# The 64-row halves of a contraction ordered one by one, in an attention and gated-MLP block

## The chip, the cores and the metric

The kernel runs on one core of a Trainium2 chip. The metric is the device time of one execution in microseconds (us), and lower is better. Before the change three executions took 269.1, 269.65 and 269.99 us; the median is 269.65.

The engines have short names in the profile. PE is the matrix engine (PEld is its loading of weights), ACT does activations and copies, DVE and POOL do vector work, and SP issues most of the DMAs. An engine works through its own instructions in order and waits on semaphores for the others.

## The reference

The computation is one transformer block with 2048 positions (S) of width 448 (D): sliding-window attention with 16 heads of 28, and then a gated MLP whose gate mixes positions.

```python
mod = silu(c) @ w_mod                     # six vectors: sa, ca, ga, sb, cb, gb
h = layernorm(x) * (1 + ca) + sa
q, k, v = split(h @ wqkv)                 # 16 heads of 28
p = softmax(q @ k.T * 28 ** -0.5)         # window of 256, causal
x = x + ga * ((p @ v) @ wo)
h = layernorm(x) * (1 + cb) + sb
z = gelu(h @ w_in)                        # 1792 wide: z1 and z2, 896 each
g = w_sp @ layernorm(z2) + b_sp           # w_sp is 2048 x 2048
x = x + gb * ((z1 * g) @ w_out)
```

What matters here is that three products contract over D = 448: Q, K and V from `wqkv`, z1 and z2 from `w_in`. 448 is three times 128 and one half of it, 64.

## The kernel before

**How 448 rows lie in 128 partitions.** The transposed activations `hT` and the weights are kept in four chunks of 128 rows that start at rows 0, 128, 192 and 320 (`CH`). Chunks 1 and 2 overlap by 64 rows. A product over all 448 rows takes chunks 0 and 3 whole, and then either chunk 1 whole with the upper half of chunk 2 (rows 64 to 127), or chunk 2 whole with the lower half of chunk 1 (rows 0 to 63). So each contraction is three matmuls of 128 rows and one half of 64.

**Two ways to do the half.** For Q, K and V the function `project` (line 775) makes, with its inner `chain`, four matmuls of 128 rows each; the half's other 64 weight rows are set to zero (`z_v`, `z_wq`), so that the fourth matmul is a padded full one. For z1 and z2 the class `Pair` (line 734) takes two contractions together, one of either kind, does six full matmuls, and one operation `rest` that issues both halves one behind the other: one on rows 64 to 127 and one on rows 0 to 63 of the array (`tile_position` (64, 0) and (0, 0)). There are 30 such pairs: 16 for z2 (448 columns, one pair per tile of 128 positions) and 14 for z1 (512 columns).

**Tile sizes on PE.** A matmul uses the array as one 128x128 tile, as two of 64x128 (the halves), as four of 32x128 (the scores, of which each head contracts 28 rows) or as four of 128x32 (the product of probabilities and V, called PV). `Planner.column_tiles` (line 104) turns runs of full matmuls that stand next to 128x32 work into four 128x32 matmuls each: an operation of mode `FREE` can stand either way, a 64-row one can't and ends a run.

**The order.** The kernel describes its work as about 1,700 operations, each with the engines that may do it, what it depends on and the buffers it needs. `Planner.schedule` (line 81) doesn't decide anything when the kernel is built: it reads the order, the engine of each operation and its buffer from a stored string (`ORDER`, line 177). A token `135/2` is operation 135 with its second free buffer choice, `.1` behind a number takes the operation's second option. `emit` then makes one instruction stream and the semaphore waits for each engine.

**The stages.** (1) Loads, layer norm, the modulation vectors; x is normed, transposed and modulated into `hT` in six blocks of 1, 1, 2, 4, 4 and 4 tiles (`BLOCKS`); blocks 0 to 2 are transposed on PE, blocks 3 to 5 by DMA from SP's queue (`transp_dma`, line 705). (2) Attention over 16 query tiles. For each there are up to three groups of 16 score matmuls (S, line 457 through `mm`), each followed by two exponentials on ACT of about 1 us (line 908), a mask on POOL (line 914) for two of three groups, PV on PE, the normalisation, and the output product with `wo`. Q, K and V of the later blocks fill PE's time between score groups, and ACT and DVE share their copies out of PSUM (lines 806, 809, 818, 821). The first z2 tiles (`zraw`, tiles 0 to 4) are also computed in this stage and copied (lines 1008, 1011). (3) z1 and z2 with their gelus on ACT and the norm of z2 on DVE and POOL. (4) The product with `w_sp` (named G here; parts of four matmuls of 512 columns), whose transposes come by DMA through SP's queue, the gating on DVE, and the output product with `w_out`. The last operation is `fin` on DVE (line 1128) and the store.

Nearly all matmuls carry line 457, and those that were split into four carry line 454, because all go through the helper `mm`.

Of the kernel before, what the change touches and what calls it, by code (L numbers as in the profile page):

```python
# [11 lines left out]
FREE, COLS, WHOLE = 128, 33, 129  # L12
# [28 lines left out]
class Op:  # L41
    __slots__ = ("name", "prio", "opts", "deps", "order", "tens", "table", "dma", "seq", "mode", "port", "accs",
                 "hold", "pair", "scores", "eng", "fn", "start", "end", "avail", "token", "extra", "pending")
# [12 lines left out]
class Planner:  # L56
# [9 lines left out]
    def op(self, name, prio, opts, deps=(), tens=(), table=None, dma=None, order=(), mode=None, port=False, accs=(), hold=500, pair=None):  # L66
        o = Op()
        o.hold, o.pair, o.scores = hold, pair, 0
        o.name, o.prio, o.opts = name, prio, opts
        o.deps, o.order, o.tens = list(flat(deps)), list(flat(order)), list(flat(tens))  # L70
        o.table, o.dma, o.mode, o.port, o.accs = table, dma, mode, port, list(flat(accs))
        o.eng, o.token, o.extra = None, None, []
        o.seq = len(self.ops)
        self.ops.append(o)
        for t in o.tens:
            t.users.append(o)
        for a in o.accs:
            a.ops.append(o)
        return o

    def schedule(self):

        for tok in ORDER.split():
# [12 lines left out]
            o.eng, _, o.fn = o.opts[int(opt or 0)]  # L96
            for a in o.accs:
# [80 lines left out]
15 0 28 23 36 35 1 2 3 21 1684/0 24 22 33 34 37/6 38 4 8 67 68 27 32 1685 1686 25 1687 1688 1689 1690 39 1691 26 69 70 6 71/2 74/7 1692 31 40/6 41 42  # L178
43 44 45 63.2 1693 1694 1695 1696 1697 1698 46 47 48 62.2 58.1 49 50 65.1 51 52 53 11 54 125 60.1 55 56 78/2 79 1699 1700 75 1701 126 127 1702 7 61
76/1 5 72/6 73.1 1703 77 1704 1705 128 95/2 129 130.1/2 85/6 86 10 90/7 12 91 180 57.1 92 96 97 87 88 93 182 181 80/4 81 98 82 94 9 99 64.2 83 183  # L180
133/1 131/3 132.1 89 59.2 84 115/4 184 134 105/5 106 107 100/6 101 13 108 109 249 14 66.1 116 117 118 30.1 119 140/1 141 142 143 247 144 250 185 186
18 188.1/0 496/0,0 498/4 135/2 136 137 138 139.1 165/3 166 167 168 102 103 104 150/1 151 152 153 155/2 156 157 158 110/1 19 111 112 113 17 145/0 146
169 160/3 161 251 147 148 154 170/1 162 163 114 245 159 497/1,1 252 190/2 248 246 253 16 149 171 187.1/4 328 20 332 254 255 164 192/3 501/8 172 173
174 189 259/3 191.1 193 194 257.1/1 120/6 121 122 123 124 513/0,1 514/5 175/1 176 517/7 258.1/0 177 178 179.1 515 333 494/3 411 215/0 216 217 218 219
256.1/4 195/2 196 197 198 199 225/1 226 227 228 229 495 520/0,1 523/2 230/0 521/9 231 232 233 234.1 220/1 221 222 205/2 206 207 208 209.1 200/3 334
263 223 502 503/0 201 202 203 29 204 499 500 504/0 210/2 211 335 261 224 505 534/1,0 518 262 330 535/10 212 213 214.1 538/3 240/3 241 242 243 235/1
236 260 244.1 264 267 516/0 265 237 238 519 524 239 266 331 541/0,1 506.1/0 329 336 522 542/2 525/0 526 337 338 340.1/1 415 268/2 545/6 323/1 324 269
278/3 279 280 281 282 344 416 546 342.1/4 346 325 326 536 548/1,0 549/4 551/1 339.1/2 327.1 270 271 341.1/3 507/0 527.1/0 288/3 289 543 343 272.1 290
417 303/0 291 304 305 306 562/0,1 566/5 292.1 563/9 413 273/1 274 275 276 283/2 539 284 285 286 307.1 277 287.1 308/3 309 569/0,1 570/8 310 311 312.1
298/1 299 300 301 418 576/0,2 547/0 540 573/7 567 537 544 552 550 302.1 293/1 414 294 577/0 564 579/1 295 296 590/1,0 528/2 553/0 554 529/0 530 531  # L190
591/4 532 297.1 508/1 509 510 511 597/1,2 594/6 571 533 580/0 568 574 598/10 575 565 572 578 345 555.1/0 556/2 601/0 512 557/1 581/0 582 348.1 558 559
604/0,1 560 561 349.1 347.1 376/0 350.1 377 378 592 583.1/0 379 380.1 361/1 605/8 618/2,0 362 363 928 959 364 607/5 595 584/2 599 619/2 381/0 622/3
382 383 384 625/2,1 365.1 412 419 366/1 367 960 368 369 602 385.1 606/0 600 626/9 420 421 423.1/2 425.1/1 370.1 596 593 603 608 609/0 610 926 929
632/2,0 627 927 629/7 635/5 633/6 611.1/0 429 427 585/1 586 587 588 356/0 646/0,1 589 963 357 650/10 318/1 647/4 422.1/3 319 320 321 322.1 358 359
360.1 653/1,2 396/1 612/2 397 398 399 400.1 943/0 944 945 946 947 948 949 950 657/1 620 660/2,0 957 313/1 951 424.1/4 654/8 314 315 316 648 961 623
624/0 621 636 634 661/0 674/1,2 317.1 663/3 658 630 631 628 962 351/1 352 353 651 354 637/0 655 656/0 662 652 638 426 639.1/1 678/7 681/2,0 675/5 676
682/0 664 659 685/1 428 432.1 430.1 649 355.1 371/1 372 373 374 665/0 688/2,1 689/6 640/1 641/0 642 643 433.1 644 683 375.1 386/1 387 388 389 958
691/9 702/2,0 706/10 645 401/0 402 403 390.1 679 703/3 404 406/1 407 408 709/0,1 964 965 966 409 405.1 613/0 614 615 616 710/4 410.1 666 454/1 455
1419 716/0,2 431 456 457 686 931 967 713/2 974/1 617 680/0 687 980 692 719/8 677 684 936 690 975 717/9 458.1 730/1,2 667.1/0 693/0 707 694 391/1 392
932 393 394 933 395.1 970/2 449/0 450 451 668/1 938 452 453.1 731/7 737/1,0 732 464/1 981 465 466 467 468.1 968/0 734/6 735 669/0 670 671 672 741/1  # L200
744/0,2 969 695.1/1 704 444/1 673 445 446 733/0 738/0 747/5 745/7 447 448.1 736 748 758/2,1 696/0 742 743 434/1 982 762/6 739 935 1423 740 759/0 746
714 435 436 437 749/0 750 763 751.1/0 711 765/1,0 769/7 770 697/0 698 699 700 1421 438.1 937 766/1 459/1 460 461 701 986 972/1 772/0,2 773/5 705/0 720
718 708 715 712 767 775/9 462 987 786/0,1 721/0 439/0 440 441 442 971 790/4 463.1 479/1 480 481 793/2,1 722 723.1/1 443.1 771/0 768 482 774 764 760
791 724/2 984 761 776 787/10 794/3 800/2,0 797/8 803/7 483.1 484/1 985 485 486 939 487 788 983 988 989 777/0 778 488.1 469/0 470 471 472 814/1,0 752/0
753/1 473.1 941 801/1 754 755 756 818/5 821/0,2 795 779.1/1 973 815/0 979 976.1 725/0 726 727 728 825/9 757 798 780/1 781/1 990 782 783 784 819 822/6
1005 828/2,1 831/2 729 804/0 792 816 785 474/1 475 476 477 1003 1004 826 993/2 823 829/4 842/1,0 846/7 930 942 1007 478.1 934 940 789 843/10 977.1 799
802 796 805/0 952/1 849/0,2 850/1 1008 1420 832/0 820 830 853/4 806 807.1/1 953 827 817 824 833/0 856/0,1 978.1 851 1072/0 1074 1073 997/0 1056/2
857/2 995/1 847 854 994 808/1 809/3 810 811 812 1058 956 859/8 1057 991/2 870/1,0 871/5 1422 955 872 954 1076/1 1077 834 1075 813 1078 1062/3 874/0
# [989 lines left out]
```

## Time and profile before

| | |
|---|---|
| executions | 269.1, 269.65, 269.99 us |
| span of the profiled execution, first to last instruction | 267.2 us |
| median over that span (the profiled execution's time outside the span isn't shown separately) | 2.45 us |
| PE busy | 258.8 us (97%), 3059 matmuls |
| ACT, DVE, POOL busy | 133.2, 166.0, 103.8 us |
| granted PE clock | 1.0 of full speed throughout |
| DMA | 23.83 MB |

A busy time is a share of the whole span, an average over stages. The views that the prediction uses are: the busy times; the chain that ended last (followed back from the last instruction, with start and length of each piece); the busy times of each engine in stretches of the span; the timeline, which lists runs of equal instructions with their start; and the groups, with the number of instructions, their busy time and the mean of one. A matmul's listed duration contains its way through the array; the next one can start long before it ends, so what a matmul costs is read from the distance of starts.

### The profile page before, as it was taken

What the parts mean: (1) busy time and instruction counts of PE and PEld (TensorE: products, weight loads), DVE (VectorE), ACT (ScalarE), POOL (GpSimd) and SP (SyncE); (2) the same over time, 40 slices, a digit from 0 to 9 for tenths busy, and PEclk for the clock granted to TensorE, in tenths of its full rate; (3) what the DMA queues carried; (4) which work ended last, traced back from release to release, by engine and by line L of the source; (5) the groups of instructions that cost most, each with busy time, mean ns of one, the idle gap of its engine ahead of it and who ended that gap; (6) DMA issues with size and microseconds to landing.
All of it is one profiled execution on the core that took longest, in us unless ns stands there. A gap on an engine that the chain in (4) does not pass through costs nothing.

```text
span 267.2 us, 7093 instructions
## 1 busy us (share of the span) xinstructions
PE 258.8 (97%) x3059; PEld 127.8 (48%) x3059; DVE 166.0 (62%) x389; ACT 133.2 (50%) x182; POOL 103.8 (39%) x163
## 2 busy tenths in 40 slices
PE   6799999999999899999999999999999999999996
PEld 2676455554554444544444444444444444444553
DVE  4789987878789999488888730722033071327553
ACT  4899899999999999977687100000000000000100
POOL 3774799997989866436532300000000000000000
PEclk9999999999999999999999999999999999999999
DMA  6974260371998341789799950000000000000133
GB/s 225 352 194 56 42 178 5 71 122 23 172 212 195 65 100 39 124 118 164 157 191 215 165 97 0 2 0 0 0 0 2 0 0 0 2 0 17 52 101 108
DMA packets 61020, 23.83 MB, mean 89 GB/s; under 512 B 49854, under 2 KB 60861, under 8 KB 60989
## 3 DMA queue, kind: packets, MB, share of 16 engines
q1 hardware_dynamic: 60715, 22.92, 41.0%
q8 instruction: 24, 0.39, 0.7%
q10 hardware_dynamic: 274, 0.46, 0.5%
q14 instruction: 7, 0.06, 0.1%
HBM read 9.47 MB, written 1.84 MB: 42 GB/s over the span
## 4 chain that ended last, share of the span: by engine, by line
PE 76%; ACT 14%; DMA 3%; DVE 3%; SPq 1%; POOL 1%; issue 1%
PE ps L457 71%; ACT PT L908 12%; PE ps L454 5%; DMA wqk_raw<-in_A_wqkv_dram 2%; DMA hT<-xn 2%; ACT QKT L806 1%; DVE w_out_sb L964 1%; POOL PT L914 1%; ACT hT L683 1%; SPq L488 1%; DVE oq L940 1%; DVE oT L949 0%; PE ps L772 0%; POOL xn L620 0%; SPq L505 0%
## 5 line engine op out<-in xcount | busy, mean ns | idle before, releaser
L908 ACT ACTIVATE PT<-ps 128x1024 bf16<-128x1024 f32 x90 | 84.5, 1059 | 2.3 <-PE ps L457 1.7
L1037 ACT ACTIVATE z1T<-ps 128x512 bf16<-128x512 f32 x28 | 15.1, 599 | 100.9 <-PE ps L457 100.8
L1106 DVE TENSOR_TENSOR tmpg<-ps,bsp_bc 128x512 bf16<-128x512 f32 x28 | 18.8, 688 | 60.9 <-PE ps L457 60.6
L457 PE MATMUL ps<-QKT,z 128*128 128x512 bf16 x224 | 50.0, 379 | 0.0
L914 POOL TENSOR_SCALAR_AFFINE_SELECT PT<-PT 128x512 f32<-128x512 f32 x60 | 36.8, 635 | 5.1 <-ACT PT L908 5.1
L457 PEld LDWEIGHTS ps<-QKT,z 128*128 128x128 bf16 x224 | 21.9, 98 | 26.4 <-ACT z2raw L1018 0.2
L607 POOL TENSOR_TENSOR rs_all<-ve_all,neghalf 128x1 f32<-128x1 f32 (+2 forms) x27 | 18.6, 692 | 27.8 <-DVE ve_all L606 26.7
L457 PE MATMUL ps<-w_spC,z 128*128 128x512 bf16 x112 | 25.8, 379 | 0.0
L457 PE MATMUL ps<-w_spD,z 128*128 128x512 bf16 x112 | 25.8, 379 | 0.0
L457 PE MATMUL ps<-hT,w_in_sb 128*128 128x512 bf16 (+1 forms) x101 | 25.2, 380 | 0.0
L457 PE MATMUL ps<-w_in_sb,hT 128*128 128x448 bf16 (+1 forms) x110 | 24.4, 353 | 0.4 <-DVE oq L940 0.2
L620 POOL TENSOR_SCALAR xn<-x_sb,rs_all,nm_all 128x512 bf16<-128x512 bf16 x26 | 20.2, 782 | 4.7 <-DVE nm_all L611 3.0
L457 PE MATMUL ps<-w_out_sb,z1T 128*128 128x448 bf16 (+2 forms) x119 | 21.9, 341 | 0.0
L457 PE MATMUL ps<-hT,WQK 128*128 128x512 bf16 (+2 forms) x123 | 21.1, 307 | 0.7 <-ACT QKT L806 0.7
L599 DVE BATCH_NORM_STATS2 st_all<-x_sb 128x6 f32<-128x448 bf16 x32 | 19.3, 615 | 3.0 <-DMA x_sb<-in_A_x_dram 2.8
L599 DVE BATCH_NORM_STATS2 st_all<-z2raw 128x6 f32<-128x448 bf16 x32 | 19.3, 618 | 2.1 <-ACT z2raw L1018 1.8
L457 PE MATMUL ps<-QKT 28*128 28x128 bf16 x720 | 18.3, 217 | 1.5 <-ACT PT L908 1.4
L457 PEld LDWEIGHTS ps<-QKT 28*128 28x128 bf16 x720 | 10.4, 92 | 15.6 <-ACT PT L908 11.3
L809 DVE CAST QKT<-ps 128x512 bf16<-128x512 f32 (+2 forms) x26 | 16.1, 624 | 2.8 <-PE ps L457 1.8
L457 PEld LDWEIGHTS ps<-w_spC,z 128*128 128x128 bf16 x112 | 10.9, 98 | 13.4 <-DVE ve_all L606 0.4
L457 PEld LDWEIGHTS ps<-w_spD,z 128*128 128x128 bf16 x112 | 11.0, 98 | 13.2
L457 PEld LDWEIGHTS ps<-w_out_sb,z1T 128*128 128x128 bf16 x119 | 11.6, 98 | 9.9
(93 smaller groups left out, 319.3 us busy)
## 6 DMA issues: line engine op xcount, KB each, us to landing
wmod_sb<-in_w_mod_dram SPq DMA_DIRECT2D x8, 224.0 KB, 4.3
w_in_sb<-in_B_w_in_dram SPq DMA_DIRECT2D x8, 224.0 KB, 4.3
out_dram<-fin SPq DMA_DIRECT2D x16, 112.0 KB, 1.7
x_sb<-in_A_x_dram SPq DMA_DIRECT2D x3, 448.0 KB, 6.6
bsp_bc<-in_B_b_sp_dram SPq DMA_DIRECT2D x1, 512.0 KB, 4.7
wqk_raw<-in_A_wqkv_dram SPq DMA_DIRECT2D x1, 452.0 KB, 5.6
wmod_sb<-in_w_mod_dram SPq DMA_DIRECT2D x1, 448.0 KB, 4.5
wmod_sb<-in_w_mod_dram ACTq DMA_DIRECT2D x1, 448.0 KB, 4.8
```

The source lines that it names most:

```text
L454: last = e.matmul(out_[32 * j:32 * j + 32], lhsT=lhsT[:, 32 * j:32 * j + 32], rhs=rhs, start=st, stop=sp, tile_position=(0, 32 * j), **kw)
L457: return e.matmul(out_, lhsT=lhsT, rhs=rhs, start=st, stop=sp, **kw)
L488: return load(name, prio, lambda e: e.dma_start(x_sb[:, t0:t0 + n, :], x_d[:, t0:t0 + n, :]), n * 128 * D * 2, order=order)
L599: st = [dve("%sst%d" % (name, i), prio, dve_ns(D), lambda e, i=i, s_=s_: e.bn_stats(st_all[:, slot, t, i, :], s_()), deps, tens) for i, s_ ...
L607: r = pool(name + "rs", prio, 420 + 148 * n, lambda e: e.tensor_tensor(rs_all[:, slot, t0:t1], ve_all[:, slot, t0:t1], neghalf[:, t0:t1], ...
L620: return e.tensor_scalar(dst, src, rs_all[:, slot, t:t + 1], nm_all[:, slot, t:t + 1], ALU.mult, ALU.add)
L683: last = e.activation(d, s_, ACT.Identity, bias=a, scale=k)
L809: return e.tensor_copy(QKT[:, g, cols], ps[:, ten.slot, 0:w])
L908: e_op = P.op("E%d_%d" % (j, ui), pr, [("act", 925, lambda e, e_in=e_in, e_out=e_out: e.activation(e_out(), e_in(), ACT.Exp, scale=SCALE)) ...
L914: ready = pool("M%d_%d" % (j, ui), pr - 50, pool_ns(512), lambda e, pt=pt, pat=pat, cm=cm, cmp=cmp: e.affine_select(out=pt32(pt.slot), in_ ...
L1037: g = P.op("z1g%d_%d" % (tb, ft), pr - 19, [("act", act_ns(512), lambda e: e.activation(z1T[:, ft, tb * 512:(tb + 1) * 512], ps[:, ten.slo ...
L1106: a = dve("ga%d_%d" % (tb, ft), pr, dve_ns(512), lambda e, tb=tb, ten=ten, tg=tg: e.tensor_tensor(tmpg[:, tg.slot, :], ps[:, ten.slot, :], ...
```

## The change

`Pair` goes. A new function `chunks` makes the three full matmuls and the half of one contraction as four operations, and each half (`rest`) is one operation by itself, for z1 and z2 and also for Q, K and V of blocks 2 to 5. There the half has two options, a padded full matmul (`whole`) and a 64-row one (`rest`); the stored order picks one of them. A full matmul or half now waits for its own chunk of `hT` and of the weights, where `Pair` waited for all. The operations are numbered anew, and the stored order is another one throughout, on all engines and in SP's queue: it also places z1's last column groups, the copies' engines, the masks and the loads differently.

In the built program 21 of the 46 padded halves of Q, K and V in blocks 2 to 5 (14 of 32 for Q and K, 7 of 14 for V) are 64-row matmuls.

```diff
-    class Pair:
...
-            def rest(e):
-                mm(e, out_ap(0), stat_a(2, slice(64, 128)), mov_a(2, slice(64, 128)), acc[0].first is r[0], acc[0].last is r[0], tile_position=(64, 0))
-                return mm(e, out_ap(1), stat_b(1, slice(0, 64)), mov_b(1, slice(0, 64)), acc[1].first is r[0], acc[1].last is r[0], tile_position=(0, 0))
...
+    def chunks(name, prio, side, opts, deps, stat, mov, n, joint=None, idx=0, rprio=None, padded=False):
...
+        for c_ in (0, 3, 1 + side):
+            o = [None]
+
+            def fn(e, c_=c_, o=o):
+                return mm(e, out_ap(), stat(c_, slice(0, 128)), mov(c_, slice(0, 128)), acc.first is o[0], acc.last is o[0])
+            o[0] = pe("%s_%d" % (name, c_), prio, mm_ns(n), fn, deps(c_), [ten], order=ops[:1], accs=[acc])
+            ops.append(o[0])
+        c_, rows, pos = (2, slice(64, 128), (64, 0)) if side == 0 else (1, slice(0, 64), (0, 0))
+        r = [None]
+
+        def rest(e):
+            return mm(e, out_ap(), stat(c_, rows), mov(c_, rows), acc.first is r[0], acc.last is r[0], tile_position=pos)
+
+        def whole(e):
+            return mm(e, out_ap(), stat(c_, slice(0, 128)), mov(c_, slice(0, 128)), acc.first is r[0], acc.last is r[0])
+        r[0] = P.op(name + "_r", prio if rprio is None else rprio, [("pe", mm_ns(n), f) for f in ([whole] if padded else []) + [rest]],
+                    [deps(c_), padded or []], [ten], order=ops[:1], mode=(FREE, 64) if padded else 64, accs=[acc])
+        ops.append(r[0])
+        return ops, ten
...
+                elif b >= 2:
+                    ops, ten = chunks("qk%d_%d" % (b, g), p_, g // 4, B_D, lambda c_, u=u, g=g: [t_wqkp[u // 2][3][(g // 4, c_)], hT_op[b][c_]],
+                                      lambda c_, r, g=g: WQK[r, c_, 4 * g:4 * g + 4, :].rearrange("p a b -> p (a b)"), lambda c_, r: hT[r, c_, cols], w, padded=[z_wq[g // 4]])
+                    proj[b].extend(ops)
...
+            else:
+                ops, ten = chunks("v%d" % t, p_, 0, B_D, lambda c_: [t_wv[c_ // 2], hT_op[b][c_]],
+                                  lambda c_, r, t=t: hT[r, c_, t * 128:(t + 1) * 128], lambda c_, r: wv_sb[r, c_, :], D, padded=[z_v])
+                proj[b].extend(ops)
...
+            pair = [chunks("z2m%d_%s" % (t, "ab"[i]), zp, i, B_D if raw else None, lambda c_, t=t, i=i: [h2_op[t][c_], t_win[4 + 2 * i + c_ // 2]], hst,
+                           lambda c_, r, i=i: w_in_sb[r, c_, FH + i * D:FH + (i + 1) * D], D, joint=joint, idx=i, rprio=zp + 0.005) for i in range(2)]
...
+                for i in range(2):
+                    ops, ten = chunks("z1m%d_%d" % (tb, f0 + i), zp, i, opts, h2d, wst1(f0 + i), hmv, 512, rprio=zp + 0.005)
+                    z1g(f0 + i, ten, [ops])
...
-15 0 28 23 36 35 1 2 3 21 1684/0 24 22 33 34 37/6 38 4 8 67 68 27 32 1685 1686 25 1687 1688 1689 1690 39 1691 26 69 70 6 71/2 74/7 1692 31 40/6 41 42
...
+1 2 0 34 36 67 68 32 69 35 3 4 8 11 6 7 22 24 23 25 29 21 1714/0 33 28 1715 1716 1717 1718 1719 37/2 1720 38 1721 40/4 41 42 43 39 44 45 46 47 48 27
...
```

More of the change, by code (lines that the diff above doesn't have):

```diff
@@ L42 @@
     __slots__ = ("name", "prio", "opts", "deps", "order", "tens", "table", "dma", "seq", "mode", "port", "accs",
-                 "hold", "pair", "scores", "eng", "fn", "start", "end", "avail", "token", "extra", "pending")
+                 "hold", "pair", "scores", "modes", "eng", "fn", "start", "end", "avail", "token", "extra", "pending")
 def flat(x):
@@ L182 @@
[L182 to L185, printed above, removed]
```

190 lines of the change are left out of this document (83 added, 107 removed).

## The prediction

> **What bounds the kernel now.** I read the busy times first, then the chain that ended last, then the busy times by stretch, then PE's timeline where it changes tile size.
>
> ```profile
> PE 258.8 (97%) x3059; PEld 127.8 (48%) x3059; DVE 166.0 (62%) x389; ACT 133.2 (50%) x182; POOL 103.8 (39%) x163
> PE 76%; ACT 14%; DMA 3%; DVE 3%; SPq 1%; POOL 1%; issue 1%
> ```
>
> PE looks like the bound of everything, but 97% is an average. The chain and the stretches (columns: PE, PEld, DVE, ACT, POOL busy us with counts, granted clock, DMA share, GB/s) split it.
>
> ```profile
> 13.28 0.92 ACT PT L908
> ...
> 28.65 5.51 PE ps L457 x68
> 34.18 5.63 ACT PT L908 x6
> 39.83 8.45 ACT PT L908 x9
> ...
> 69.51 13.86 ACT PT L908 x15
> ...
> 116.76 147.88 PE ps L457 x726
> ```
>
> ```profile
> 12.00:22.00 10.00, 9.59 (x175) 6.69 (x171) 8.98 (x23) 9.93 (x25) 7.96 (x13) 1.00 0.80 189
> 22.00:34.00 12.00, 11.83 (x256) 6.17 (x248) 11.00 (x29) 10.50 (x14) 7.22 (x10) 1.00 0.25 48
> 34.00:48.30 14.30, 14.27 (x344) 7.39 (x332) 11.48 (x28) 14.16 (x17) 13.73 (x21) 1.00 0.31 83
> 48.30:69.50 21.20, 21.18 (x477) 11.52 (x481) 17.02 (x38) 21.11 (x23) 19.21 (x28) 1.00 0.47 97
> 69.50:83.50 14.00, 13.03 (x322) 6.79 (x318) 11.74 (x27) 13.99 (x16) 12.64 (x20) 1.00 1.05 185
> 83.50:105.50 22.00, 20.98 (x426) 10.37 (x430) 20.50 (x45) 20.98 (x24) 16.19 (x25) 1.00 0.41 92
> 105.50:113.00 7.50, 7.50 (x185) 3.96 (x178) 3.97 (x13) 7.14 (x9) 4.28 (x7) 1.00 0.60 95
> 113.00:149.00 36.00, 35.92 (x228) 15.62 (x221) 31.73 (x85) 25.96 (x39) 14.58 (x24) 1.00 0.95 171
> 149.00:240.00 91.00, 91.00 (x423) 41.26 (x422) 28.67 (x60) 0.92 (x1) 1.81 (x3) 1.00 0.10 16
> ```
>
> From 34 to 83.5 us ACT works 49.26 of 49.5 us: the exponentials set the pace and PE only has to keep up. Before 34 and from 83.5 to 105.5 both engines have small holes (ACT idles 1.57 and 1.02 us). From 105.5 on PE alone sets the time. So an extra PE microsecond costs full price late, part price around the exponentials, and little in the middle.
>
> **The change, part by part.** Prices of PE come from its timeline (start, us, group):
>
> ```profile
> 122.46 0.59 PE L457 MATMUL ps<-hT,w_in_sb 128*128 128x512 bf16 x2
> 122.89 0.35 PE L457 MATMUL ps<-w_in_sb,hT 128*128 128x448 bf16 x1
> 123.08 1.13 PE L457 MATMUL ps<-hT,w_in_sb 128*128 128x512 bf16 x6
> ...
> 127.80 1.13 PE L457 MATMUL ps<-w_in_sb,hT 128*128 128x448 bf16 x6
> 128.77 0.38 PE L457 MATMUL ps<-hT,w_in_sb 128*128 128x512 bf16 x1
> ```
>
> ```profile
> 110.69 0.37 PE L454 MATMUL ps<-w_in_sb,hT 128*32 128x448 bf16 x4
> 111.00 0.36 PE L457 MATMUL ps<-w_in_sb,hT 64*128 64x448 bf16 x2
> 111.20 0.38 PE L457 MATMUL ps<-hT,w_in_sb 64*128 64x512 bf16 x2
> 111.51 0.37 PE L454 MATMUL ps<-w_in_sb,hT 128*32 128x448 bf16 x4
> 111.71 0.29 PE L457 MATMUL ps<-PT,Vaug 128*32 128x128 bf16 x8
> ```
>
> Starts tell the pitch: two 512-column matmuls take 122.89 - 122.46 = 0.43, so 0.216 each; one of 448 takes 123.08 - 122.89 = 0.19. Two 64-row halves of 448, on the upper and lower rows, take 111.20 - 111.00 = 0.20 together: a pair costs what one matmul does. The pair of 512 before a wave of 128x32 takes 111.51 - 111.20 = 0.31, and the four 128x32 of 448 before the 64-row pair take 0.31 instead of the 0.20 that the next such wave takes (111.71 - 111.51). So every change of tile size costs about 0.097, in and out. The six instructions at 127.80 confirm it: two full matmuls around two pairs are four slots, 0.76, and last 0.97, which leaves 0.21 for two changes.
>
> (1) Padded halves of Q, K and V. Counting the built programs, 21 of the 46 padded 128-row matmuls of blocks 2 to 5 go (11 of 512 columns, 3 of 256, 7 of 448): 11 x 0.216 + 3 x 0.108 + 7 x 0.19 = 4.0 us less.
>
> (2) The halves, now ordered one by one. Before, the 60 halves of z1 and z2 stand in 30 pairs: 14 x 0.216 + 16 x 0.19 = 6.1. After, 81 halves stand as 32 pairs with a partner on the other rows (22 hold a 512, 9 are of 448, 1 of 256) and 17 alone (6, 10 and 1): 28 x 0.216 + 19 x 0.19 + 2 x 0.108 = 9.9. That is 3.8 more. No lone half stands in this trace. Its price lies between 0.10 (half a slot) and 0.216 (a slot). I take the slot, because the pair above lasts as long as one half of it must: two start together and the next group starts 0.2 later. At the lower end 17 x 0.1 = 1.7 us would go. The Trainium skill ("TensorE: Matmul & The Clock Gate", Why this matters for your kernels) says that a lone matmul of few rows takes as long as one of 128 and that only concurrency gains; by it the sum below stands, by half a slot it would be 1.7 lower, and no run here shows a lone half.
>
> (3) Tile changes. Consecutive matmuls of different tile size go from 119 to 154: 35 x 0.097 = 3.4 more. Unlike a pair, a lone half pays one or two changes for itself.
>
> PE's sum is -4.0 + 3.8 + 3.4 = +3.2 us. By stage, counted between the same score (S) groups: +0.5 until 34 us, +1.5 from there to 83.5, +1.1 from there to 105.5, and 0.0 afterwards (one more pair slot and two changes, against work that was done earlier).
>
> (4) ACT. Its part of the copies changes (groups: busy us, mean ns, idle before; the last row is POOL's mask, used under 5):
>
> ```profile
> L806 ACT ACTIVATE QKT<-ps 128x128 bf16<-128x128 f32 x15 | 3.2, 282 | 0.3 <-PE ps L772 0.3
> L806 ACT ACTIVATE QKT<-ps 128x256 bf16<-128x256 f32 x5 | 1.6, 405 | 0.3 <-PE ps L457 0.3
> L806 ACT ACTIVATE QKT<-ps 128x512 bf16<-128x512 f32 x2 | 1.2, 600 | 0.3 <-PE ps L454 0.3
> L1011 ACT ACTIVATE z<-ps 128x448 bf16<-128x448 f32 x3 | 1.6, 544 | 0.0
> L722 ACT ACTIVATE WQK<-wqk_raw 128x512 bf16<-128x512 bf16 x2 | 1.3, 626 | 2.3 <-DMA wqk_raw<-in_A_wqkv_dram 2.3
> L722 ACT ACTIVATE WQK<-wqk_raw 64x256 bf16<-64x256 bf16 x3 | 1.1, 409 | 0.1
> L914 POOL TENSOR_SCALAR_AFFINE_SELECT PT<-PT 128x512 f32<-128x512 f32 x60 | 36.8, 635 | 5.1 <-ACT PT L908 5.1
> ```
>
> Two Q/K copies of 128 columns (-0.43) and two of 256 (-0.64) go, one of 512 comes (+0.6), the third V copy moves up by 0.54 from the end, and two more z2 copies stand between the first and the last exponentials (+1.1, one of them from behind). From first to last block of exponentials ACT gets about 0.8 us more. Before the first Q/K copies four 64x256 spreads of weights (1.6) now stand in one row behind the hT copies, where one stood on DVE and two ran in a wait for DMA: the first exponential comes 0.3 to 0.5 later.
>
> (5) Queues. SP now issues the four block-3 transposes ahead of the last x load, and POOL does four masks ahead of the last xn (three more than before). Timeline of what that feeds:
>
> ```profile
> 19.72 0.77 POOL L620 TENSOR_SCALAR xn<-x_sb,rs_all,nm_all 128x512 bf16<-128x512 bf16 x1
> 25.94 1.38 DVE L697 TENSOR_SCALAR hT<-hT,modT 128x512 bf16<-128x512 bf16 x4 [0.58 <-DMA hT<-xn]
> ```
>
> Three masks of 0.635 are 1.9 us, partly done early; PE reaches block 3 some 0.7 us of work later than before, and the x load no longer shares DMA with the transposes. I cost it at 0.2; uncovered it is up to 1.2. DVE loses six 512-column modulations and POOL gets them: nothing, as POOL is 39% busy, but a late one holds PE in order. The order from 149 us on is new, too, with the first G part that needs the last norm of z2 12 parts, 12 x 4 x 0.216 = 10.4 us, behind the last z2 matmul; that covers the norm, so nothing (if DVE, 31.73 of 36 us busy there, falls behind: up to 0.8). The last stores wait for the same final fin: nothing.
>
> **Sum.** Until 34 us PE +0.5 beside ACT +0.3: +0.5 (0 to 1.2). From 34 to 83.5 ACT has the same exponentials and PE +1.5: +0.2 (0 to 1.5). From 83.5 to 105.5 PE +1.1, ACT +0.55, both near full: +0.8 (-0.3 to 1.3). Then 0.1 (-0.2 to 0.8). Together +1.6 (-0.5 to +4.8). The profiled span is 267.2; the three runs are 269.1 to 269.99, the median 269.65, 2.45 above the span, which I take for what lies around it. 269.65 + 1.6 = 271.25.
>
> **Rivals.**
> Hidden anyway: ACT's pace covers PE's extra in all three attention stages, and only 0 to 0.8 remains: 270.0. For it: ACT's 49.26 of 49.5. Against: at 28.65 and from 83.5 the chain is on PE.
> PE's full price: the +3.2 is paid, since scores are computed just ahead of their exponentials and a drain falls between them, with a new wait or two: 272.9 to 273.9. Against: PE's slack beside ACT.
> Faster: the new order fills ACT's holes. Its idle time from 12 to 34 and from 83.5 to 105.5 is 1.57 + 1.02 = 2.6; less its own 0.8, 1.8 is to be had: 267.9. It decides if score groups in both stretches are ready before ACT asks. PE's extra work there speaks against it.
> Halves at half price: a lone half lasts 0.1 and pairs form across contractions, so the halves are worth their 21 padded slots: -4.0 + 3.8 - 1.7 = -1.9, if the changes fall in waits for ACT: 267.7. The pair's 0.20 speaks against it.
> The Trainium skill ("TensorEngine Tiling (Array Packing)", Theoretical Speedup) promises up to twice the speed for a contraction of 64 rows or fewer; by it alone the 21 would save half of 4.0, an estimate of 267.6. The trace agrees for two halves issued together, and no run here shows it for one.
>
> **How the numbers follow.** Forecast 0.53, hidden 0.19, full price 0.16, filled holes 0.08, half price 0.04. The forecast's own range is 270.2 to 272.6. Within 0.3% (0.8 us, about what a measurement here can tell from no change) lie the hidden case and the forecast's low edge: 0.23; faster 0.12; slower 0.65. The range 268.5 to 273.6 leaves out most of the two fast cases and the worst of the full price.
>
> **What would show it.** PE's lone 64-row matmuls: next start 0.2 to 0.3 later, not 0.1. More 0.1 us gaps between tile sizes. Spacing of score groups from 34 to 83.5 as before, about 1.85 us for two exponentials (13.86 for 15). The last score group about 1.5 us later, and PE's time after it as long as before. Wrong if the first exponential comes earlier than 13.28, if the late G parts wait for z2, or if lone halves cost less than a slot.

## The result, and the profile after

Four executions of the changed kernel took 271.63 to 273.0 us, median 272.44; four of the kernel before on the same chip 269.1 to 269.99, median 269.69. The ratio is 1.0102, 95% interval 1.0079 to 1.0124: the change costs 2.75 us. On two other occasions it came out at 1.0100 (1.0068 to 1.0132) and 1.0115 (1.0092 to 1.0138). The forecast was 271.2 with a range of 268.5 to 273.6, and 65% for slower.

One thing has to be known before two profiles are laid side by side. In every execution whose span is listed with its time, the time is 1.7 us above the span. The profiled execution of before has a span of 267.2, so it was one of about 268.9, which is 0.75 faster than the median. The prediction took 2.45 us for "what lies around" the span; 1.7 of it is that, and 0.75 is that the profiled execution was a fast one. The profiled execution after took 273.0, with a span of 271.3, and is the slowest of its four. So the difference of the two profiles, 4.1 us, is more than what the change costs. Of before there is one profile and of after there are three; two kernels derived from before (`delay_b3` and `split_dense` below) do the same work in the attention stage and give a second look at it. One execution of all runs, at 275.86 us 1.6% above the fastest of its kernel, was in a slower state and is left out.

The busy times and the shares of the chain, after:

```profile
PE 263.0 (97%) x3044; PEld 128.0 (47%) x3044; DVE 168.6 (62%) x392; ACT 133.5 (49%) x180; POOL 104.4 (38%) x162
PE 90%; DVE 6%; DMA 2%; issue 1%; ACT 1%; DVEq 0%; SPq 0%
```

The stretches of after, cut where a score group begins (columns as in the prediction: PE, PEld, DVE, ACT, POOL busy with counts, granted clock, DMA share, GB/s):

```profile
35.51:72.29 36.78, 35.74 (x825) 18.70 (x825) 31.54 (x70) 35.87 (x39) 31.53 (x46) 1.00 0.50 112
72.29:87.33 15.04, 14.70 (x345) 7.06 (x344) 13.27 (x29) 14.91 (x17) 11.28 (x17) 1.00 0.60 114
87.33:109.15 21.82, 21.27 (x404) 10.05 (x404) 19.18 (x40) 21.16 (x25) 18.02 (x26) 1.00 0.51 102
...
117.00:153.00 36.00, 36.00 (x234) 16.07 (x229) 31.78 (x89) 25.86 (x40) 13.82 (x22) 1.00 0.99 173
153.00:244.00 91.00, 91.00 (x427) 41.43 (x426) 29.08 (x62) 1.08 (x2) 2.13 (x4) 1.00 0.01 3
```

And those of before, cut at the same three groups:

```profile
33.73:69.06 35.33, 35.28 (x807) 18.80 (x807) 28.40 (x64) 35.20 (x39) 32.77 (x48) 1.00 0.40 90
69.06:83.51 14.45, 13.47 (x339) 7.14 (x339) 12.12 (x28) 14.35 (x17) 13.09 (x20) 1.00 1.04 185
83.51:105.33 21.82, 20.81 (x414) 10.19 (x415) 20.32 (x45) 20.97 (x24) 16.03 (x23) 1.00 0.42 93
```

The chain has changed sides: ACT had 14% of it and has 1%; PE has 90%. Stage by stage, after less before: the stage up to the first cut took 35.51 instead of 33.73, +1.8; the first stretch 36.78 instead of 35.33, +1.45; the second 15.04 instead of 14.45, +0.6; the third 21.82 both times. Behind it PE is full in both kernels, and the stage got 0.2 longer (159.30 us from the last cut to the last matmul, where before had 159.06).

**How the attention stage is read.** Between the first and the last cut lie 74 exponentials. Back to back they start 0.904 us apart, in both kernels, and 74 of them make 66.9 us. What the stage takes beyond that is lateness (an exponential starts later than 0.904 behind the one before, with no other ACT work between) and the copies that ACT does between two exponentials; any wait behind such a copy is counted with the copies. Read from the starts of ACT's instructions, in us:

| kernel | stage | 74 x 0.904 | lateness: 1st stretch, 2nd, 3rd | copies |
|---|---|---|---|---|
| before | 71.60 | 66.9 | 0.98, 0.12, 1.54 | 2.07 |
| after | 73.64 | 66.9 | 2.43, 0.58, 1.02 | 2.71 |
| after, second profile | 73.67 | 66.9 | 2.47, 0.58, 1.02 | 2.71 |
| after, third profile | 73.44 | 66.9 | 2.25, 0.57, 1.02 | 2.71 |

The parts are defined so that they make up the stage, but for 0.02 at its ends. Attention got 1.84 to 2.07 longer: 1.2 to 1.4 by later exponentials and 0.64 by copies (four stand there, all of z2, where before had two of z2 and one of V). The kernel `delay_b3`, whose attention does the same as before's, takes 71.59 there with a lateness of 2.65; `split_dense` takes 72.38, with one stall of PE of 0.66 at 57 us. Less than half of the added lateness shows in ACT's idle time (1.08 us of the stage before, 1.44 to 1.70 after), because an exponential that starts late overlaps less with its neighbour, and that counts as busy time. A run of 18 exponentials across the second stretch, before and then after (start, length; no idle time is marked in either):

```profile
68.37 16.83 ACT L908 ACTIVATE PT<-ps 128x1024 bf16<-128x1024 f32 x18
```

```profile
71.60 17.21 ACT L915 ACTIVATE PT<-ps 128x1024 bf16<-128x1024 f32 x18
```

The same 18 take 0.38 longer without a hole. The Trainium skill ("ScalarE: Activation LUTs", What ACT_TABLE_LOAD costs) says that back-to-back activations overlap by about 93 ns. The runs agree in kind and show more: an exponential that had to wait lasts 1.02, and the next one starts 0.904 to 0.92 behind it, which is an overlap of 0.1 to 0.12.

Who is late is told by what ends the wait of PE's weight loads, listed for 34 to 105 us; "issue" means that nothing in the profile held them. Before, and then after (columns: total, times, longest):

```profile
PEld ps L457 <- ACT PT L908: 10.2, 25, 0.6
PEld ps L457 <- issue: 1.7, 5, 0.4
```

```profile
PEld ps L460 <- issue: 10.3, 35, 0.4
PEld ps L460 <- ACT PT L915: 5.6, 14, 0.6
```

Before, a score group stood ready 25 times and waited for the exponential that frees its buffer: PE was ahead. After, that happens 14 times, and 35 times the weights were loaded as soon as PE came to them: PE was behind. Over each kernel's own stage, from the first cut to the last, the counts are 27 and 5 before, 16 and 34 after.

### The profile page after: what moved, and what is told of

It is laid out like the page before. It is cut to its first block, busy times and chain, and to the rows that moved or that the text cites. A ratio compares the mean times of both kernels' runs of the same rounds, so it can differ in the third digit from the quotient of the medians.

```text
span 271.3 us, 7057 instructions
## 1 busy us (share of the span) xinstructions
PE 263.0 (97%) x3044; PEld 128.0 (47%) x3044; DVE 168.6 (62%) x392; ACT 133.5 (49%) x180; POOL 104.4 (38%) x162
## 3 DMA queue, kind: packets, MB, share of 16 engines
HBM read 9.47 MB, written 1.84 MB: 42 GB/s over the span
## 4 chain that ended last, share of the span: by engine, by line
PE 90%; DVE 6%; DMA 2%; issue 1%; ACT 1%; DVEq 0%; SPq 0%
PE ps L460 83%; PE ps L457 7%; DMA hT<-xn 1%; DVE oq L947 1%; DMA x_sb<-in_A_x_dram 1%; DVE QKT L811 1%; DVE hT L700 1%; PE ps L770 0%; DVE st_all L602 0%; DVE Vaug L828 0%; DVE w_out_sb L971 0%; DVE xn L623 0%; DVE nm_all L614 0%; ACT hT L686 0%; ACT QKT L808 0%
## 5 line engine op out<-in xcount | busy, mean ns | idle before, releaser
L915 ACT ACTIVATE PT<-ps 128x1024 bf16<-128x1024 f32 x90 | 85.4, 1032 | 2.9 <-PE ps L460 1.9
L460 PE MATMUL ps<-w_in_sb,hT 128*128 128x448 bf16 (+1 forms) x113 | 28.5, 354 | 0.1
L460 PE MATMUL ps<-w_spC,z 128*128 128x512 bf16 x112 | 26.8, 379 | 0.0
L460 PE MATMUL ps<-hT,w_in_sb 128*128 128x512 bf16 (+1 forms) x100 | 26.5, 380 | 0.0
L460 PE MATMUL ps<-hT,WQK 128*128 128x512 bf16 (+4 forms) x130 | 23.2, 305 | 0.7 <-DVE mv_all L605 0.5
L1124 DVE TENSOR_TENSOR fin<-ps,x_sb 128x448 bf16<-128x448 f32 (+2 forms) x17 | 9.8, 594 | 18.4 <-PE ps L460 15.2
L623 POOL TENSOR_SCALAR xn<-x_sb,rs_all,nm_all 128x512 bf16<-128x512 bf16 x24 | 18.6, 778 | 3.0 <-DVE nm_all L640 1.6
L811 DVE CAST QKT<-ps 128x512 bf16<-128x512 f32 (+2 forms) x29 | 17.1, 598 | 3.2 <-PE ps L460 1.7
L700 POOL TENSOR_SCALAR hT<-hT,modT 128x512 bf16<-128x512 bf16 (+1 forms) x21 | 15.7, 755 | 5.9 <-DMA hT<-xn 5.9
L460 PE MATMUL ps<-PT,Vaug 128*32 128x128 bf16 x720 | 17.5, 221 | 0.0
```

The lines of the kernel that those rows point to most:

```text
L460: return e.matmul(out_, lhsT=lhsT, rhs=rhs, start=st, stop=sp, **kw)
L623: return e.tensor_scalar(dst, src, rs_all[:, slot, t:t + 1], nm_all[:, slot, t:t + 1], ALU.mult, ALU.add)
L700: return e.tensor_scalar(hT[:, c_, cols], hT[:, c_, cols], modT[:, base_col + 4 + c_:base_col + 5 + c_], modT[:, base_col + c_:base_col + ...
L811: return e.tensor_copy(QKT[:, g, cols], ps[:, ten.slot, 0:w])
L915: e_op = P.op("E%d_%d" % (j, ui), pr, [("act", 925, lambda e, e_in=e_in, e_out=e_out: e.activation(e_out(), e_in(), ACT.Exp, scale=SCALE)) ...
L1124: fs.append(dve("fin%s%d" % (nm, t), pr, dve_ns(c1 - c0), lambda e, t=t, ten=ten, ft_=ft_, c0=c0, c1=c1: e.tensor_tensor(fin[:, ft_.slot, ...
```

## The experiments

"Counted work" is the sum over PE's instructions by the pitches of the prediction (0.216 and 0.19 a slot, 0.097 a tile change), without waits. The kernel before took 269.77, 269.56 and 269.67 us in the three series, and each ratio is to it. The times of one kernel within a run of six lie 0.7 to 2.7 us apart, so a difference of less than 1 us between two of the changed kernels is not settled by their medians alone.

**The changed kernel again.** No edit; a second profile, and the base of the first series.

> The changed kernel once more, beside the three kernels that are derived from it. Both theories: about 272.4 us, 1.010 of the kernel before. Its score groups should again lose 3 to 4 us until 109 us and nothing afterwards; if the loss of 1.2 us ahead of block 3 (25 to 30 us) is chance, it should differ here by more than 0.5 us.

Measured: 272.82 us, 1.0100 (1.0068 to 1.0132). The late start and the longer attention stage are there again (rows of the table above); the last score group comes 3.8 us later than before's. PE's two waits ahead of block 3 are 1.03 us together, where the first profile has 1.55, the third 1.17 and before 0.17: some of that wait is chance, most of it is not. PE's matmuls from the last cut to the last one took 159.05, against 159.06 before: the stage in which PE alone counts is the same.

**What a lone half and a tile change cost.** Timeline of after, around one lone half, and around three V matmuls of which the middle one is the half:

```profile
56.90 0.38 PE L457 MATMUL ps<-hT,WQK 128*32 128x512 bf16 x4
57.22 0.39 PE L460 MATMUL ps<-hT,WQK 64*128 64x512 bf16 x1
57.53 0.62 PE L457 MATMUL ps<-hT,WQK 128*32 128x512 bf16 x8
...
83.58 0.95 PE L460 MATMUL ps<-wv_sb,hT 128*128 128x448 bf16 x3
84.36 0.38 PE L460 MATMUL ps<-hT,WQK 128*128 128x512 bf16 x1
```

The half of 512 columns starts 0.32 behind the group before it and holds up the next by 0.31; both are a slot of 0.216 and a change of 0.097. The three V matmuls take 0.78: three slots of 0.19 and two changes make 0.76. So a lone half among full matmuls costs 0.41 where the padded one cost 0.216. To show the changes by themselves, a kernel was made of before in which the visits to the 64-row size behind the last score group are cut in pieces, by moving a full matmul of z between two pairs; nothing else moves, and the tile changes go from 119 to 145. One of the cuts, with two changes, lies ahead of the last PV matmul; the other 24 changes lie behind it.

```diff
-... 1296 1377/1 1198 1368 1374 1294 1293 1372 ...      # four pairs, then four full matmuls
+... 1296 1294 1377/1 1293 1198 1372 1368 1374 ...      # a full one between two pairs
```

> The old kernel with the visits to 64-row tiles after the last score group cut apart: 26 visits instead of 13, the same 30 pairs, the same work, 26 more changes of tile size, all where PE alone sets the time. At 0.097 us a change it is 2.5 us slower (272.2). If the gap at a change is filled with other work elsewhere, less than 1.

Measured: 272.49 us, 1.0096 (1.0072 to 1.0120). A pair of 512 columns that now stands alone:

```profile
133.76 0.39 PE L455 MATMUL ps<-hT,w_in_sb 64*128 64x512 bf16 x2
134.08 1.25 PE L455 MATMUL ps<-w_in_sb,hT 128*128 128x448 bf16 x6
```

It holds up the next matmul by 0.32, one slot and one change. From the last PV matmul to the last one of z2 this kernel takes 38.97 us and before 36.43: +2.55, for 24 changes, which is 0.106 each. From the last score group to the last matmul it is +2.76 for all 26, again 0.106. So the price is a tenth above the 0.097 of the prediction, and where PE is the only bound it is paid in full. The medians differ by 2.9; the stall at 57 us is in this profile as well.

**The halves without the new order.** The order of before, engine by engine and buffer by buffer, with the z pairs as they were; only the same 21 halves of Q, K and V are 64-row matmuls, each where its padded one stood. It is written with after's `chunks`, so that a matmul waits for its own chunk; ACT, DVE, POOL and SP have the same instructions in the same order as before.

```diff
-... 437 ...
+... 437.1 ...      # the half's second option; 21 such tokens
```

> The old order, engines and buffers, instruction for instruction, with the z halves in their old pairs; only the same 21 halves of Q, K and V are 64-row matmuls where their padded ones stood. 157 changes of tile size instead of 119, 38 x 0.097 = 3.7 us more PE work, all before 105 us (1.4 until 34 us, 2.0 from there to 83.5, 0.3 after); a half itself costs the slot that it had. Theory 'price paid': 2.8 to 3.7 us slower than the kernel before, about 273.0. Theory 'ACT covers 34 to 83.5': 1.3 to 2.0 slower. Were a lone half worth half a slot, it would be 2 us less than either.

Measured: 272.10 us, 1.0087 (1.0066 to 1.0109), which is 2.5 more than before and lies between the two theories; run again in the third series, 272.30, 1.0090 (1.0071 to 1.0110). All 21 stand alone there (157 tile changes), so the counted work is 3.7 us more than before. In the two profiles attention takes 73.16 and 73.43, with 4.06 and 4.31 of lateness: +1.6 and +1.8 for 2.3 of counted work in that stage. The waits of PE's weight loads:

```profile
PEld ps L458 <- issue: 10.2, 32, 0.4
PEld ps L458 <- ACT PT L913: 7.2, 18, 0.8
```

PE is behind 32 times instead of 5. ACT was at work for nearly all of this stage before, and that gave PE no cover: PE was just ahead of it, and each slot and change that it gets more makes scores late by most of its size.

**The new order without the halves.** After, with all 21 halves of Q, K and V padded again; z1 and z2 stay as the change has them. Counted work is 1.3 less than after's and 1.8 more than before's, with 131 tile changes.

```diff
-... 437.1 ...
+... 437 ...        # 21 tokens
```

> The changed order with all 21 halves of Q, K and V padded again: 131 changes of tile size instead of 154, 21 more full matmuls. Counted at the pitches (0.216 and 0.19 us a slot, 0.097 a change), PE's work falls by 1.3 us: nothing until 55 us, 1.2 of it between 72 and 87 us. Theory 'PE's price is paid nearly everywhere': 271.1 us (0.9 to 1.6 below the changed kernel). Theory 'ACT's exponentials cover PE between 34 and 87 us': less than 0.4 below it.

Measured: 272.09 us, 1.0087 (1.0056 to 1.0118), 0.7 less than after in the same series, again between the two theories. Attention takes 73.75 (lateness 2.44, 0.55 and 0.96, copies 2.90), which is no less than after's, though PE has 1.4 us less counted work there (67.9 instead of 69.3). Its weight loads:

```profile
PEld ps L458 <- ACT PT L913: 7.6, 18, 0.8
PEld ps L458 <- issue: 5.2, 15, 0.4
PEld ps L458 <- DVE QKT L809: 1.8, 5, 0.5
PEld ps L458 <- DVE Vaug L826: 1.8, 2, 1.2
PEld ps L458 <- DVE oq L945: 1.2, 4, 0.5
```

So the new order costs about as much by itself as the halves do by themselves (2.3 and 2.5 us in the medians), and both together little more than one of them (2.75 to 3.5). What holds PE in the new order is seen in the waits of its matmuls, 34 to 105 us, before and then in this kernel:

```profile
PE ps L457 <- DVE oq L940: 0.2, 1, 0.2
```

```profile
PE ps L458 <- DVE Vaug L826: 1.1, 2, 0.7
PE ps L458 <- DVE mv_all L603: 0.7, 1, 0.7
PE ps L455 <- DVE QKT L809: 0.2, 1, 0.2
```

PE waits 2.0 us for DVE here, 1.2 in after, 0.4 in the kernel with the halves alone and 0.2 before. The waits of its weight loads for DVE grew less (5.2 us before, 6.2 here). No run takes these waits away, so it is argued and not shown that they make the new order late.

**Half of the mid-stage repaired.** After, with the nine lone halves between 35 and 87 us padded; 1.64 us less counted work, 137 tile changes.

```diff
-... 321.1 ... 354.1 ... 482.1 ... 487.1 ...
+... 321 ... 354 ... 482 ... 487 ...      # nine tokens
```

> The changed kernel with only the nine lone halves between 35 and 87 us (v6, v11, v13, v14 and five of Q and K) padded: 17 changes of tile size fewer, 1.6 us less PE work, all of it in the stretch where ACT ran nearly full before. Theory 'PE's price is paid there too': 1.2 to 1.7 us faster than the changed kernel, about 271.0. Theory 'ACT covers it': within 0.4 of the changed kernel, and the score groups at 87 us no earlier.

Measured: 272.84 us, 1.0104 (1.0075 to 1.0132), nothing gained on after's 272.82. The profile has a stall that no other has at this place, in the middle of the 48 PV matmuls of a group, with nothing that releases it:

```profile
92.58 0.53 PE L458 MATMUL ps<-PT,Vaug 128*32 128x128 bf16 x23
94.12 0.57 PE L458 MATMUL ps<-PT,Vaug 128*32 128x128 bf16 x25 [1.02 <-issue]
```

The same kernel again, beside after:

> The changed kernel with the nine lone halves between 35 and 87 us as padded full matmuls, a second time, because the first profile of it had one stall of 1.02 us with no releaser in the middle of a group of PV matmuls, at 93 us, which no other profile has there. PE's counted work is 1.64 us less than after. Theory A (PE's extra work is paid in this stage, and the first run lost its gain to the stall and to scatter): median 1.0 to 1.7 us below the changed kernel of the same chip, and the last score group that much earlier. Theory B (ACT and DVE set the pace there, so PE's work is covered): within 0.4 us of the changed kernel, and the waits of PE grow by 1.2 us or more without the stall.

> The changed kernel, as the measure for the three runs beside it. Both theories: median 272.2 to 273.0 us, ratio to the kernel before 1.008 to 1.012.

Measured: 272.19 us against 273.16 of after, 0.97 less, with single times from 271.29 to 273.99. That lies between what the two theories say. The profile decides more, as its stall is gone: attention takes 73.22 (after's third profile beside it: 73.44) for 1.64 less counted work, and PE's waits grew by 1.04 up to the end. In the second stretch PE has 1.15 us less to do and gains 0.04. This shows where it went (that kernel, and then after's third profile):

```profile
85.17 0.61 DVE L826 CAST Vaug<-ps 128x448 bf16<-128x448 f32 x1
85.84 0.93 PE L458 MATMUL ps<-wo_sb,oT 128*128 128x448 bf16 x4 [0.66 <-DVE Vaug L826]
...
71.02 15.91 ACT L913 ACTIVATE PT<-ps 128x1024 bf16<-128x1024 f32 x17
87.16 1.02 ACT L913 ACTIVATE PT<-ps 128x1024 bf16<-128x1024 f32 x1 [0.22 <-PE ps L458]
```

```profile
85.43 0.61 DVE L828 CAST Vaug<-ps 128x448 bf16<-128x448 f32 x1
86.10 0.93 PE L460 MATMUL ps<-wo_sb,oT 128*128 128x448 bf16 x4 [0.23 <-DVE Vaug L828]
```

With the halves padded, 15 exponentials in a row start 0.904 apart; then PE stands 0.66 us for a V copy on DVE, which frees the buffer of the output product, and the next exponential is 0.52 late at once. With the lone halves the same lateness comes in small pieces (0.05 to 0.2 at several places), and PE waits 0.23 for the copy. By the traces DVE's copy sets the end of this stretch in both; no run moves that copy.

**All lone halves padded.** Twelve instead of nine; 135 tile changes, 1.83 us less counted work than after.

> The changed kernel with twelve halves of Q, K and V padded (the nine, and three more before 35 us and behind 87 us); PE's counted work is 1.83 us less than after, the changes of tile size 135 instead of 154. Theory A: 1.2 to 1.9 us below the changed kernel. Theory B: 0 to 0.6 us below.

Measured: 272.13 us over five executions, 1.0094 (1.0067 to 1.0122), 1.03 less than after: between the bounds of the two theories. Its profile is not read.

**The halves alone, second run.** Its expectation, for the comparison within one series:

> The order of before with the same 21 halves as 64-row matmuls, a second time, to set the price of the halves against the price of the new order. If the new order costs by itself (late block 3, waits on DVE): 0.3 to 0.9 us below the changed kernel. If the new order only spares PE work (counted: 0.6 us less than this kernel): 0.3 to 0.6 us above the changed kernel.

It is 0.86 below after, as the first alternative has it: the new order spares 0.6 us of PE work against this kernel and still ends later. The halves alone came out lower in each comparison (1.0087 and 1.0090, after 1.0100 to 1.0115), but the intervals overlap.

**The wait at block 3.** After's beginning, up to the first cut, is 1.6 to 1.8 later than before's; 0.5 of it is counted work. Most of the rest is in one place. Before, and then after (`ve_all` is the variance of the block's tiles, SPq the four transposes in SP's queue, L697 and L700 the modulation of `hT`, of which before's row is in the prediction):

```profile
15.21 0.17 DVE L606 TENSOR_SCALAR ve_all<-mv_all 128x4 f32<-128x4 f32 x1
17.15 5.92 SPq L705 DMA_TRANSPOSE hT<-xn  x4
...
26.41 0.40 PE L454 MATMUL ps<-hT,WQK 128*32 128x512 bf16 x4 [0.17 <-DVE hT L697]
```

```profile
16.80 0.16 DVE L609 TENSOR_SCALAR ve_all<-mv_all 128x4 f32<-128x4 f32 x1
18.73 6.07 SPq L708 DMA_TRANSPOSE hT<-xn  x4
21.66 0.77 POOL L623 TENSOR_SCALAR xn<-x_sb,rs_all,nm_all 128x512 bf16<-128x512 bf16 x1
27.40 1.44 DVE L700 TENSOR_SCALAR hT<-hT,modT 128x512 bf16<-128x512 bf16 x3 [1.77 <-DMA hT<-xn]
27.87 0.37 PE L457 MATMUL ps<-wv_sb,hT 128*32 128x448 bf16 x4 [1.22 <-DVE hT L700]
28.58 0.37 PE L457 MATMUL ps<-wv_sb,hT 128*32 128x448 bf16 x4 [0.33 <-DVE hT L700]
```

The variance is ready 1.59 later, the first transpose starts 1.58 later, and the modulation 1.46 later; PE, which before waited 0.17, waits 1.22 and 0.33. The last normed tile is not to blame: POOL ends it at 22.43, while the four transposes go one behind the other in SP's queue, 1.25 to 2.15 us each, and the chain has the last one begin at 23.53. Two experiments were made on it. The first adds a delay to before: three unused statistics on DVE ahead of the block's variance.

```diff
+    for q in range(3):
+        dve("wait%d" % q, 0, 600, lambda e, q=q: e.bn_stats(st_all[:, 0, 4 + q, 1, :], x_sb[:, 4 + q, :]), [t_x[4]])
```

> The old kernel with three more statistics of 0.55 us (results unused) on DVE ahead of block 3's, which makes these and the transposes 1.6 us later, as they are in the changed kernel; PE's work is the same. Theory 'a late block 3 stays lost': PE waits 1.0 to 1.6 us longer at 26 us and the kernel is 0.9 to 1.6 us slower (270.9). Rival 'the holes of ACT and PE up to 105 us take it back': less than 0.5 slower.

Measured over 12 executions: 270.10 us, 1.0017 (1.0003 to 1.0031), which is 0.5 more than before and between the theory and its rival. In the profile the variance of block 3 is ready 1.56 later and the first transpose starts 1.55 later, as intended, but PE doesn't wait for block 3 at all. It waits earlier, where before doesn't, for the modulation of block 2, which stands behind the added statistics on DVE:

```profile
19.64 1.49 PE L455 MATMUL ps<-hT,WQK 128*128 128x256 bf16 x12 [0.66 <-DVE hT L686]
```

The score groups come 0.87 later at 23 us, 0.79 later at 29 us, and stay 0.8 later to the end. So of 1.6 us taken on DVE about half is lost, and what is lost before 30 us is not caught up by the exponentials; that the late transposes of block 3 cost anything by themselves is not shown. The size is unsure, too: two profiles of the halves alone, with nothing changed between them, differ by 0.8 at the same place, and one of them has a wait of 0.38 for the same modulation.

Ahead of that variance DVE has more to do than before: one of the norms, and three copies of block 1's Q and K, of which ACT did all three before (it has taken over one that DVE did). The second experiment gives these back to ACT.

```diff
-... 144.1 ... 169.1 ... 174.1 ...
+... 144 ... 169 ... 174 ...       # three copies on ACT
```

> The changed kernel with three copies of K and Q of block 1 (qke1_3, qke1_4, qke1_7) on ACT instead of DVE, so that DVE reaches the statistics of block 3 about 0.8 us earlier and the four transposes start earlier. PE's work is the same. Theory 'late statistics hold PE ahead of block 3': PE's wait of 1.2 us there shrinks to 0.2 to 0.6, and the time falls by 0.5 to 1.0 us (about 271.7). Rival 'the masks ahead of the last norm on POOL hold it', as predicted: no earlier transposes, the same wait. Rival 'ACT is the bound there': three copies of 0.2 us more on ACT, 0.6 slower.

Measured: 273.47 us, 1.0121 (1.0092 to 1.0151), slower than after. The wait at block 3 is gone (PE waits 0.08 us between the two score groups around it, where after waits 1.95), and another has come earlier:

```profile
15.11 1.97 ACT L806 ACTIVATE QKT<-ps 128x128 bf16<-128x128 f32 x9
...
19.93 0.74 PE L458 MATMUL ps<-wv_sb,hT 128*128 128x448 bf16 x3 [1.41 <-ACT QKT L806]
```

Against the first exponential the variance is 0.6 earlier than in after, but the first transpose only 0.1 (5.29 us behind that exponential, where after has 5.38 to 5.39). So PE's wait is gone because PE itself comes later, and the run doesn't tell what an earlier block 3 would be worth. ACT has no room there either: its copies now stand between the first two exponentials, and the score groups behind them come up to 3.8 later than before's; 2.7 of that is left at the first cut, where after has 1.8. The last experiment does both repairs, the three copies on ACT and the twelve lone halves padded:

> The changed kernel with both repairs: the three copies on ACT, and the twelve lone halves of Q, K and V padded (nine that stand in pairs stay). PE's work is 1.8 us less than in the changed kernel and 1.3 more than in the old one. Theory 'price and late block 3 explain the loss': 269.7 to 270.6, within 0.3% of the kernel before. If something else in the new order costs as much, it stays above 271.

Measured: 272.19 us, 1.0100 (1.0068 to 1.0132). That is above 271: the price of the lone halves and the late block 3, as far as these edits mend them, do not explain the loss. The kernel has 1.3 us more counted work than before and is 2.6 us slower. Attention takes 73.28, of which 3.58 is lateness.

No version came out that beats before. What the prices point to is fewer visits to the 64-row size in the stage where PE alone counts. There a visit of four pairs holds all eight accumulators that the order knows (0 to 7), and four of before's eight visits behind the last score group are such already; nothing of this kind was tried.

## Why the prediction was right, and where it was not

**Sign and size.** Forecast 271.2, measured 272.44: the right side, inside the range, 1.2 too low. The likeliest case had its own range to 272.6. With the span's offset of 1.7 in place of 2.45 and a typical execution of before (269.69 less 1.7, 268.0), the terms stand as they were; the sum of +1.6 is to be held against +2.75. In the profiles the terms miss by more: the start and the next 50 us together came to 2.8 to 3.1 us more than forecast, the stretch behind them to 0.8 less, and the profile of before is of an execution 0.75 faster than the median. That the total misses by no more than 1.2 is in part luck. Of the signs that the prediction named, PE's time behind the last score group held; that group came 3.4 to 3.8 us later and not 1.5, and the score groups from 34 to 83.5 us did not keep their spacing.

**(1) to (3), PE's count: right.** -4.0, +3.8 and +3.4 came to +3.2. Counted by the built programs with the pitches, it is +3.10. The lone half costs a slot, as taken: 0.31 to the next start, where half a slot would have made 0.20. That closes the rival of half price. The Trainium skill ("TensorE: Matmul & The Clock Gate", Why this matters for your kernels) says of 32 rows that a lone matmul takes as long as one of 128; the trace shows the same for 64, with that 0.31. The factor of two that the Trainium skill ("TensorEngine Tiling (Array Packing)", Theoretical Speedup) gives holds here for two halves issued together (0.20 for both) and not for one. A tile change was taken as 0.097; 24 of them measured 0.106 each, which adds 0.3 us to the count.

**Start, +0.5 (0 to 1.2): too low; (5) named the wrong cause.** Up to the first cut it is +1.6 to +1.8, of which executions that differ in nothing may account for up to 0.8. Counted work is 0.5 of it, as said. The prediction put the risk on POOL's masks ahead of the last normed tile; that tile was 1.1 us early. What is late by the trace is DVE's statistics, as DVE has more work ahead of them (one norm and two copies net), and then four transposes in a row; neither of the two runs made on it isolates that. The step costed DVE's side at nothing because of what DVE lost; it should have asked what stands on DVE ahead of the first transpose.

**34 to 83.5, +0.2 (0 to 1.5): wrong, the step that failed.** It said "the exponentials set the pace and PE only has to keep up". Measured over the first two stretches: +1.8 to +2.1. ACT's 49.26 of 49.5 us busy was read as cover for PE, and it is none. Up to 69.5 us the rows that the prediction shows have PE busy for 14.27 of 14.30 and 21.18 of 21.20 us beside it, so busy time could not tell which of the two had room. PE was ahead of ACT by less than one exponential (the longest wait of a weight load for ACT was 0.6 us), a late one shows in good part as busy time, and what is lost once is never made up, since ACT has no slack to catch up with. The halves alone made this stretch later by 1.4 to 1.7 for 2.0 of counted work. In the new order it is not PE's work alone: with 1.6 less of it these stretches are no more than 0.2 to 0.4 shorter, and waits for DVE stand in the traces in its place. So "hidden anyway" (270.0) fails.

**83.5 to 105.5, +0.8 (-0.3 to 1.3): measured 0.0.** Copies cost 0.64 more here, close to the 0.55 that the sum has for ACT, and lateness went down by 0.52 (1.54 to 1.02): the new order does fill holes, but only in this stretch. The rival "filled holes" was right about that and about nothing else.

**After that, +0.1: right.** 0.0, 0.1 and 0.2 in three profiles; the late G parts don't wait for z2.

**The rival of full price** (272.9 to 273.9) lies as near as the forecast, and its sum is nearly what was paid: 3.1 counted, 2.75 measured. Its reason, that scores are computed just ahead of their exponentials, is the one that the waits of the weight loads show. But the new order without the halves is as late in attention, so that the two amounts agree is in part chance.

What stays open: why the new order's first stretch, without the halves, is late by 2.4 with as much counted work as before's, which is late by 1.0. In after two of the larger latenesses of this stretch (0.4 each, at 46 and 67 us) come 1.5 us behind a wait of PE for DVE (0.54 at 44 and 0.50 at 65 us), and the kernel without the halves has these two waits as well (0.70 and 0.39); the others were not traced. Nor is it shown what makes the single stalls without a releaser.

## What to carry to other kernels

An engine that is 99% busy in a stage gives the engines that feed it no cover unless they are ahead by more than one of its instructions: read the starts of its instructions against the closest spacing they reach, and see which engine ends the feeder's waits. A matmul of half the rows is worth its while only beside another one on the other rows and in a visit of several; alone it costs a full slot and two tile changes, 0.41 instead of 0.22 here, and a single pair with its two changes (0.41) saves next to nothing against two padded matmuls (0.43). Before an order is changed throughout, measure the change in the old order and the new order without the change; here each alone gave most of the loss.

## What the runs showed that was not expected

- Exponentials of 1024 columns keep a spacing of 0.904 us to within a few ns, 14 times in a row, so a stage can be summed up as count times spacing, lateness and copies.
- Single stalls of PE with no releaser, inside a group of equal matmuls: 1.02 us at 93 us in one profile and in no other, and 0.66 at 57 us in the profile of the cut visits; three other profiles have smaller ones (0.18 to 0.34) within 1 us of that same score group. Two profiles of one kernel differ by up to 0.8 us near the start. One profile of a kernel is not enough to read a difference of less than 1 us.
- Two 64-row halves of 448 columns on the same rows, next to each other in after at 98.55 us, start 0.20 apart, like full matmuls; the pairs on different rows, as before at 111.00 us, start within 0.01 and share a slot.
